# Reordering splits, exponentials and weight loads in a fused attention and two-mixture kernel

## The chip, the cores and the metric

The kernel runs on one core of a Trainium2 chip. The metric is the device time of one execution in microseconds; the time of a version is the median of its runs. The engines are named as in the profile: PE (TensorE, matrix products), PEld (its weight loads), DVE (VectorE), ACT (ScalarE), POOL (GpSimd), SP (SyncE, which issues most of the transfers). "SPq" and "ACTq" are transfers issued from the queues of SP and ACT.

## What is computed

Three stages follow each other, all in float32:

```python
# attention in chunks of 64, 8 batches x 8 heads x 576 positions x 64
scores = matmul(q_c, k_c^T) / 8
attn = exp(scores - max); attn /= sum(attn) + 1e-9
x = matmul(attn, v_c)                    # laid out as 4608 tokens x 512
# first mixture: 512 -> 2048 -> 512
h = x @ w_in
x = (h * clip(h + 3, 0, 6) / 6) @ w_out
# second mixture: 512 -> 1024 -> 512
h = x @ w_in2
s = h * softmax(h)
out = (layer_norm(s) * g_ln) @ w_out2
```

## The kernel before

**Precision.** Every float32 operand of a product is split into a rounded part `hi` (a ScalarE copy into a 1-pass type) and a remainder `lo` (a subtraction `lo = x - hi`, mostly on VectorE, here and there on GpSimd). A product is then three: hi*hi, lo*hi, hi*lo. So each product waits for one copy and one subtraction.

**The work in order.** The 4608 tokens are nine blocks of 512. Attention is done in 36 units of 128 tokens, spread between the products of the first mixture.

1. Blocks 0 to 2 run plainly. `moe_h` makes one 128-row piece of h (12 products), `moe_gate_there` applies the gate, `moe_split` makes `g_hi` and `g_lo`, and `o_next` (`moe_o`, 12 products) uses the piece made before. The loop `for F in range(2 * NF)` covers blocks 1 and 2, 32 steps. In odd F up to 25 an attention slot stands (`att_slot`: scores of the next unit into the one `att` bank, the values of the last one). A unit's eight exponentials (`attn_exp_act`, line 448, which read that bank) are done four in the odd F and four in the even F after it, from `STEPS`. Meanwhile `sums_of` (lines 1075 to 1083) and `split_sums` (lines 1089 and 1090) make sums of the weights for later and store them in DRAM (`sti`, `sto`); `UNITS` says in which F.
2. Blocks 3 to 8 are three pairs, with products in Strassen's form: seven products of half size instead of eight. `pair_7` does the first two pairs, `pair` the last.
   - The first half of `pair_7` has eight steps j. Each step multiplies in the order A11, S2, S1, S3, A12, then A22 and S4 of the step before (function `finish`), each of them six products in `mul7`, line 1164. VectorE adds s1, u2 (line 1373), u3 (line 1395) and c22 (line 1397); the gate and GpSimd follow and the results go into the groups B11, T1, B22, B21 of `wo` slots. Three further sums go to DRAM (`later_t`, line 1346).
   - The second half of `pair_7` makes seven outputs i with eight steps j each (`mul_o`, line 1301), d counts pairs of them. `prepare(d + 3)` splits operands (lines 1285 and 1286), `bring(d)` loads a sum back from `later_t` (line 1295). At j = 7 of the first two outputs stands an attention slot; its loads of values, queries and keys (lines 136, 129, 130) are issued one step later from SP's queue. The splits for the next pair come from the list `prep`, one at each of ten places; the eleventh (T4 in all but the first pair) is left over in `todo` and is done in the first step of the next pair.
   - `pair`, the last one, has the same seven products per step but runs output products plainly (`o_next`), stores halves of h in DRAM (`held`) and has the conversion of the second mixture's weights between: class `Second`, whose `window(words, small, hi)` scales a chunk on ScalarE (line 155), makes its words on VectorE (lines 258, 261, 267), starts the load of the chunk after next (line 145, two buffers `xr`), does small subtractions (lines 295, 302) and starts copies (line 319). `load_o` loads the second half of the block's weights from `sto` (line 1493).
3. The second mixture follows, with products by lines 751 and 949.

**What sets the order.** The kernel is written with a manual schedule: the order in the program is the order on each engine and on each DMA queue. An instruction that waits holds all that stand behind it on its engine. The weights of the pairs come through a ring of 16 pieces (`ring_fetch`, line 1151): each `mul7` and `mul_o` takes one and issues the next load into the freed place. The PSUM bank `b` of a step of `pair` is written by S2, added to by S3 and A22, and read by u2 (line 1522), u3 (line 1533) and c21 (line 1551) between these; the bank `a` is released by ramp and gate (lines 1230 and 550).

The order at the start of a step of `pair`, with what the change moves:

```python
mul7(b, j, "S2", "T2", True, False)
u2 = work_tile("s")
nc.vector.tensor_add(out=u2, in0=s1, in1=b)
if not j:
    fill.window(1, 0)
while todo:
    todo.pop(0)()
fill.window(1, 2)
c = h_psum()
mul7(c, j, "S1", "T1", True, False)
o_next()
mul7(b, j, "S3", "T3", False, False)
```

Of the kernel before, what the change touches and what calls it, by code (L numbers as in the profile page):

```python
# [21 lines left out]
def tile_kernel(  # L22
# [12 lines left out]
    nc = tc.nc  # L35
# [1224 lines left out]
    def home(name, m):  # L1260
        return wo_slot(GROUPS.index(name) * ND + m, F32)
# [26 lines left out]
        for k in range(2):  # L1288
            parts_o[i, 2 * m + k] = [t[k] for t in e]

    def bring(d):
        i, m = divmod(d, ND)
        if 0 <= i < 3:
            t = g_t[HOMES[i], m] = home(HOMES[i], m)
            nc.sync.dma_start(out=t, in_=later_t[i, m])

    def mul_o(ps, i, j, start, stop):
        w, x = ring_take("o", OUTS[i][0], j), parts_o.pop((i, j))
# [12 lines left out]
    def pair_7(p, todo):  # L1311
# [44 lines left out]
        for j in range(NJ):  # L1356
            u = base + event[j] if j in event else NU
            n = 2 * (j % 2)
            a = acc_bank(n) if j else att_psum()[:, 0]
            mul7(a, j, "A11", "B11", True, False)  # L1360
            s1 = work_tile("s")
            nc.scalar.copy(out=s1, in_=a)
            load_coming()
            while todo:
                todo.pop(0)()
            if late:
                gate_22(late[0])
            stage("turn", u)
            stage("exp", u + 1)
            b = acc_bank(n + 1) if j else h_psum()  # L1370
            mul7(b, j, "S2", "T2", True, False)
            u2 = work_tile("s")
            nc.vector.tensor_add(out=u2, in0=s1, in1=b)
            if j % 2 == 0:
                for g in GROUPS:
                    g_t[g, j // 2] = home(g, j // 2)
            m, k = j // 2, j % 2
            if j == 1:
                made = finish(*late, lambda: stage("norm", u + 1))
# [3 lines that stand above are left out]
            o_next()  # L1383
            if j > 1:
                made = finish(*late, lambda: stage("norm", u + 1))
            if j == NJ - 1:
                prepare(0)
            if made:
                i, t, ps = made
                gate(t, ps, t)  # L1390
                later_sums(i, t)
            if j != 1:
                mul7(b, j, "S3", "T3", False, False)
            u3 = ap1.tile([P, DM], F32, tag="tx2", name="tx2")
            nc.vector.tensor_add(out=u3, in0=s1, in1=b)  # L1395
            c22 = g_t["B22", m][:, k]
            nc.vector.tensor_add(out=c22, in0=u3, in1=c)
            mul7(a, j, "A12", "B21", False, True)
            t = gp_tile("t")
            ramp(a, t)  # L1400
            o_next()
            if u < NU:
                att_slot(u, u + 2, coming)
            if j == NJ - 1:
                prepare(1)
            gate(t, a, g_t["B11", m][:, k])
            late = j, b, c, s1, u2
# [15 lines left out]
        for i in range(len(OUTS)):  # L1423
# [7 lines left out]
            for j in range(NJ):  # L1431
                mul_o(ps, i, j, i in (0, 1, 3, 6), i in (2, 4, 5, 6))
                d = (i * NJ + j) // 2
                if (i, j) == (0, 5):
                    while waiting:
                        waiting.pop(0)()
                if j % 2:
                    bring(d)
                else:
                    prepare(d + 3)  # L1440
                if (i, j) in steps:
                    todo.pop(0)()
                u = base + 6 + i
# [9 lines left out]
                if final:  # L1453
                    if (i, j) == (5, 7):
                        second.append(Second())
                    elif (i, j) in ((6, 4), (6, 7)):
                        second[0].window(1, 0, False)
                    if j % 2 and d % 2 == 0 and d > 2 * ND:
                        load_o(d // 2 - ND - 1)
            for s in range(2):  # L1460
                if i == 0:
                    nc.scalar.copy(out=s1[s], in_=a[s])
# [34 lines left out]
    def pair(p, todo):  # L1497
        b1, b2 = FIRST + 2 * p, FIRST + 2 * p + 1
        hang, fill = None, second[0]
        for j in range(NJ):  # L1500
            lastj = j == NJ - 1
            if j == 1:
                width.update({"s": 3, "xo": 3})
                fill.places.append(3)
            if 2 * ND + 1 + j < NF:
                load_o(2 * ND + 1 + j)
            a = att_psum()[:, 0]
            mul7(a, j, "A11", "B11", True, False)
            s1 = work_tile("s")
# [1 line left out]
            if hang:  # L1511
                t, f = hang
                g = moe_split(t, nc.gpsimd)
                pend.append((b1, f, g))
            for _ in todo[:-1]:
                todo.pop(0)()
            if j:
                fill.window(1, 0)
            b = h_psum()
            mul7(b, j, "S2", "T2", True, False)  # L1520
            u2 = work_tile("s")
            nc.vector.tensor_add(out=u2, in0=s1, in1=b)
            if not j:
                fill.window(1, 0)
            while todo:
                todo.pop(0)()
            fill.window(1, 2)
            c = h_psum()
            mul7(c, j, "S1", "T1", True, False)
            o_next()  # L1530
# [4 lines left out]
            nc.vector.tensor_add(out=c22, in0=u3, in1=c)  # L1535
            if not lastj:
                nc.sync.dma_start(out=held[2 * j + 1], in_=c22)
            mul7(a, j, "A12", "B21", False, True)
            if lastj:
                for n in range(4):  # L1540
# [22 lines left out]
                nc.sync.dma_start(out=held[2 * j], in_=c12)  # L1563
            fill.store()
            hang = gated(c21), 2 * j + 1
        g = moe_split(hang[0], nc.vector)
        pend.append((b1, hang[1], g))

# [105 lines left out]
    for F in range(2 * NF):  # L1674
        b, f = 1 + F // NF, F % NF
        if F == 0:
            xn[2] = new_x()
        hp, t = moe_h(f, *xn[b])
        end = F == 2 * NF - 1
        (moe_gate if end else moe_gate_there)(hp, t)  # L1680
        if F - 2 in UNITS:
# [10 lines left out]
        if F < 2 * NF - 1:  # L1692
            o_next()
        for step, u, which in STEPS.get(F, []):
            if step == "exp":
                attn_exp_act(u, which)
            elif step in ("norm", "last"):
                if step == "norm":
                    attn_norm(u)
                attn_turn(u, which)  # L1700
# [145 lines left out]
```

## Time and profile before

| | |
|---|---|
| time, median of 3 runs | 1193.73 us (1192.16 to 1196.63) |
| the profiled execution's own time | 1193.68 us |
| its span, first to last instruction | 1192.0 us |
| PE busy | 1169.7 us, 98% |
| DVE, ACT, POOL busy | 75%, 61%, 41% |
| mean granted clock of PE | 0.996 |
| DRAM and SBUF transfers | 258.6 MB, 217 GB/s on the mean |

The profile is of one execution. The span leaves out what lies around the program, 1.7 us here. Busy PE is a modelled figure: products overlap, so a product of 392 ns takes its place in a row of products that is about 230 ns apart. The granted clock is 1.0 at 2.4 GHz and 0.5 at 1.2 GHz. Rows of a timeline give start and length in us, engine, line, operation, output and inputs, and in brackets the idle time of the engine before it and what ended that. What ended it is inferred; where several things were waited for, the last one by the profile is named.

### The profile page before, as it was taken

The numbers are of one execution on the slowest core, as the hardware profiler recorded it, in microseconds if no ns is written. First come the engines' busy times: TensorE is split into PE (matmuls) and PEld (weight loads), VectorE is DVE, ScalarE is ACT, GpSimd is POOL, SyncE is SP. The second block draws the span as 40 slices with busy tenths as digits, with TensorE's granted clock in tenths as the row PEclk, the third lists the DMA queues.
The fourth block names the chain that finished last, engine by engine and source line by source line (L and its number), as shares of the span: only waits on it lengthen the run. The fifth ranks groups of instructions, "written<-read, shape, count | busy, mean of one in ns | idle before, by whom it ended". The sixth has DMA issues, their size and how long they took to land.

```text
span 1192.0 us, 21417 instructions
## 1 busy us (share of the span) xinstructions
PE 1169.7 (98%) x7199; PEld 952.9 (80%) x7199; DVE 890.2 (75%) x1415; ACT 727.9 (61%) x1669; POOL 491.5 (41%) x565
## 2 busy tenths in 40 slices
PE   8999999999999999999999899999999999999998
PEld 6888778788888778787887788888888888888887
DVE  7987667677576987577866666678887878877874
ACT  7775545555465773366644333356886867777775
POOL 1000565443066610275500112101677676765764
PEclk9999999999999999999999899999999999999999
DMA  9901767777689997799999999862322222222311
GB/s 369 381 28 62 241 212 264 239 253 252 243 281 307 313 400 239 242 311 300 336 399 345 351 361 326 306 234 81 128 73 92 79 86 85 79 92 71 99 58 61
DMA packets 172253, 258.60 MB, mean 217 GB/s; under 512 B 19056, under 2 KB 86896, under 8 KB 172144
## 3 DMA queue, kind: packets, MB, share of 16 engines
q1 hardware_dynamic: 159760, 234.69, 57.2%
q10 hardware_dynamic: 12384, 22.55, 5.4%
q8 instruction: 57, 0.93, 0.3%
q14 instruction: 52, 0.43, 0.1%
HBM read 170.40 MB, written 76.02 MB: 207 GB/s over the span
## 4 chain that ended last, share of the span: by engine, by line
PE 91%; DVE 3%; DMA 2%; POOL 1%; ACT 1%; issue 1%; SPq 1%; ACTq 0%; POOLq 0%; DVEq 0%
PE acc L574 17%; PE po L949 16%; PE hp L535 9%; PE acc L1301 9%; PE hp L1164 9%; PE acc L1164 8%; PE b L751 6%; PE c L751 4%; PE a L751 4%; PE hp L1301 3%; PE att L398 3%; PE att L1164 2%; PE att L751 1%; POOL xo L1090 1%; DMA xr<-in_moe_w_in 1%
## 5 line engine op out<-in xcount | busy, mean ns | idle before, releaser
L574 PE MATMUL acc<-g_hi,wo 128*128 128x512 f32 x640 | 163.9, 395 | 0.0
L574 PEld LDWEIGHTS acc<-g_hi,wo 128*128 128x128 f32 x640 | 119.6, 189 | 26.6
L1164 PE MATMUL hp<-wi,w 128*128 128x512 f32 x468 | 119.1, 398 | 7.1 <-ACT wi L319 6.3
L1164 PEld LDWEIGHTS hp<-wi,w 128*128 128x128 f32 x468 | 89.2, 191 | 28.2 <-issue 6.7
L1164 PE MATMUL acc<-wi,w 128*128 128x512 f32 x420 | 104.4, 395 | 2.2 <-DVE tx L1395 2.2
L864 ACT COPY wo<-wo 32x256 f32<-32x256 f32 x228 | 92.1, 404 | 19.2 <-DVE wo L846 11.3
L535 PE MATMUL hp<-x_hi,wi 128*128 128x512 f32 x384 | 97.8, 396 | 0.1
L732 POOL TENSOR_TENSOR x_lo<-xr,x_hi 128x768 fp32r<-128x768 f32 (+1 forms) x30 | 64.1, 2157 | 76.4 <-ACT x_hi L725 76.4
L1301 PE MATMUL acc<-wi,w 128*128 128x512 f32 x408 | 95.3, 392 | 0.0
L1164 PEld LDWEIGHTS acc<-wi,w 128*128 128x128 f32 x420 | 77.9, 188 | 19.5 <-DVE tx L1395 2.5
L1301 PEld LDWEIGHTS acc<-wi,w 128*128 128x128 f32 x408 | 76.5, 188 | 16.8
L448 ACT ACTIVATE p<-att,mx 128x64 f32<-128x64 f32 x256 | 76.6, 320 | 18.8 <-DVE mx L431 16.0
L574 PE MATMUL acc<-g_lo,wo 128*128 128x512 f32 x320 | 87.7, 390 | 0.0
L535 PEld LDWEIGHTS hp<-x_hi,wi 128*128 128x128 f32 x384 | 71.5, 187 | 17.1 <-ACT x_hi L512 0.3
L1286 DVE TENSOR_TENSOR wi<-wo,wi 128x1024 fp32r<-128x1024 f32 x50 | 66.2, 1344 | 24.1 <-ACT wi L1285 23.6
L1285 ACT CAST wi<-wo 128x1024 fp32r<-128x1024 f32 x50 | 51.4, 1065 | 33.4 <-PE hp L1301 16.6
L836 DVE SCALAR_TENSOR_TENSOR wo<-wo,r,wo 128x1024 f32<-128x1024 f32 x36 | 70.3, 1952 | 1.3
L574 PEld LDWEIGHTS acc<-g_lo,wo 128*128 128x128 f32 x320 | 60.1, 188 | 12.8
L933 POOL TENSOR_TENSOR wo<-wo,wo 128x1024 fp32r<-128x1024 f32 x25 | 64.5, 2582 | 6.4 <-ACT wo L929 3.8
L560 POOL TENSOR_TENSOR g_lo<-t,g_hi 128x512 fp32r<-128x512 f32 x15 | 21.4, 1428 | 106.3 <-ACT g_hi L557 98.4
L828 ACT ACTIVATE wo<-wo,nmx 128x1024 f32<-128x1024 f32 x36 | 41.5, 1152 | 22.4 <-DVE nmx L825 22.3
L541 ACT ACTIVATE t<-hp,three 128x512 f32<-128x512 f32 x48 | 33.3, 694 | 35.0 <-PE hp L535 32.4
(319 smaller groups left out, 2848.5 us busy)
## 6 DMA issues: line engine op xcount, KB each, us to landing
w<-sti SPq DMA_DIRECT2D x168, 256.0 KB, 4.8
w<-sto SPq DMA_DIRECT2D x112, 256.0 KB, 5.2
later_t<-xo SPq DMA_DIRECT2D x48, 256.0 KB, 4.6
wo<-later_t SPq DMA_DIRECT2D x24, 512.0 KB, 6.9
wo<-wo SPq DMA_DIRECT2D x328, 32.0 KB, 1.8
x2d<-xo SPq DMA_DIRECT2D x36, 256.0 KB, 4.5
xr<-x2d SPq DMA_DIRECT2D x36, 256.0 KB, 3.3
out<-ob SPq DMA_DIRECT2D x36, 256.0 KB, 2.2
```

The source lines that it names most:

```text
L448: nc.scalar.activation(out=p_t[u][:, h], in_=sc[:, c, a], func=AF.Exp, scale=0.125, bias=mx[:, m : m + 1], accum_out=sums[u][:, h : h + 1],)
L535: nc.tensor.matmul(hp, wi[f][:, a, kk * P : (kk + 1) * P], b[:, kk], start=(n == 0), stop=(n == 3 * KD - 1),)
L574: nc.tensor.matmul(acc[dc], wo[f][:, w, dc * P : (dc + 1) * P], g[i], start=(at == 0 and n == 0), stop=(at == NF - 1 and n == 2),)
L732: eng.tensor_sub(out=lo[:, f], in0=r, in1=hi[:, f].bitcast(F32))
L751: nc.tensor.matmul(ps, x[:, AT[a], j], w2[w, j][i], start=(start and n == 0), stop=(stop and n == 5), skip_group_check=True,)
L836: nc.vector.scalar_tensor_tensor(out=h, in0=e, scalar=r, in1=h, op0=ALU.mult, op1=ALU.mult, accum_out=mu)
L864: move(out=m[b * 32 : b * 32 + 32, a], in_=tr[a * 32 : a * 32 + 32, b])
L933: eng.tensor_sub(out=lo, in0=m, in1=hi.bitcast(F32))
L949: nc.tensor.matmul(po, a[f], out_w[f][w], start=(n == 0), stop=(n == 3 * NF2 - 1),)
L1164: nc.tensor.matmul(ps, w[:, i, kk * P : (kk + 1) * P], x[:, kk], start=(start and n == 0), stop=(stop and n == 5), skip_group_check=True,)
L1286: nc.vector.tensor_sub(out=e[1], in0=src, in1=e[0].bitcast(F32))
L1301: nc.tensor.matmul(ps[s], w[:, k, s * P : (s + 1) * P], x[l], start=(start and j == 0 and n == 0), stop=(stop and j == NJ - 1 and n == 2), ...
```

## The change

- In `pair_7`, first half: what is left in `todo` is done behind u2, not ahead of the second product. At j = 7 `prepare(0)` stands behind c22, not ahead of the gate and u3.
- In `pair_7`, second half: the twelve loads from `later_t` were issued one per d in d = 0 to 11. Now they stand at d = 0, 2, 4, 6 (first sum), 8, 10, 12, 14 (second) and 16 to 19 (third), by the table `BRING_AT`.
- `load_o`: in the second pair nine were issued at even d from 10 to 26; now four at d = 21, 23, 25, 27. In `pair` one per step in seven steps became two per step in six.
- In `pair`, first step: what is left in `todo` follows u2 at once; the first window moves behind c22 and its store, the second to the end of the step. In later steps nothing moves. (The loop over `todo[:-1]` had nothing to do, since one entry is left.)
- In the loop over F: the second four exponentials of a unit, in even F, stand behind `moe_h` and ahead of the gate and of `moe_split`; they stood behind `o_next`. The first four, in odd F, stay.

```diff
--- before.py
+++ after.py
@@ -1288,11 +1288,12 @@
         for k in range(2):
             parts_o[i, 2 * m + k] = [t[k] for t in e]
 
-    def bring(d):
-        i, m = divmod(d, ND)
-        if 0 <= i < 3:
-            t = g_t[HOMES[i], m] = home(HOMES[i], m)
-            nc.sync.dma_start(out=t, in_=later_t[i, m])
+    def bring(i, m):
+        t = g_t[HOMES[i], m] = home(HOMES[i], m)
+        nc.sync.dma_start(out=t, in_=later_t[i, m])
+
+    BRING_AT = {2 * m: (0, m) for m in range(ND)} | {2 * (ND + m): (1, m) for m in range(ND)}
+    BRING_AT |= {4 * ND + m: (2, m) for m in range(ND)}
 
     def mul_o(ps, i, j, start, stop):
         w, x = ring_take("o", OUTS[i][0], j), parts_o.pop((i, j))
@@ -1361,8 +1362,6 @@
             s1 = work_tile("s")
             nc.scalar.copy(out=s1, in_=a)
             load_coming()
-            while todo:
-                todo.pop(0)()
             if late:
                 gate_22(late[0])
             stage("turn", u)
@@ -1371,6 +1370,8 @@
             mul7(b, j, "S2", "T2", True, False)
             u2 = work_tile("s")
             nc.vector.tensor_add(out=u2, in0=s1, in1=b)
+            while todo:
+                todo.pop(0)()
             if j % 2 == 0:
                 for g in GROUPS:
                     g_t[g, j // 2] = home(g, j // 2)
@@ -1383,8 +1384,6 @@
             o_next()
             if j > 1:
                 made = finish(*late, lambda: stage("norm", u + 1))
-            if j == NJ - 1:
-                prepare(0)
             if made:
                 i, t, ps = made
                 gate(t, ps, t)
@@ -1395,6 +1394,8 @@
             nc.vector.tensor_add(out=u3, in0=s1, in1=b)
             c22 = g_t["B22", m][:, k]
             nc.vector.tensor_add(out=c22, in0=u3, in1=c)
+            if j == NJ - 1:
+                prepare(0)
             mul7(a, j, "A12", "B21", False, True)
             t = gp_tile("t")
             ramp(a, t)
@@ -1434,10 +1435,10 @@
                 if (i, j) == (0, 5):
                     while waiting:
                         waiting.pop(0)()
-                if j % 2:
-                    bring(d)
-                else:
+                if j % 2 == 0:
                     prepare(d + 3)
+                elif d in BRING_AT:
+                    bring(*BRING_AT[d])
                 if (i, j) in steps:
                     todo.pop(0)()
                 u = base + 6 + i
@@ -1455,8 +1456,8 @@
                         second.append(Second())
                     elif (i, j) in ((6, 4), (6, 7)):
                         second[0].window(1, 0, False)
-                    if j % 2 and d % 2 == 0 and d > 2 * ND:
-                        load_o(d // 2 - ND - 1)
+                    if j % 2 and d >= 5 * ND and d % 2:
+                        load_o((d - 5 * ND) // 2)
             for s in range(2):
                 if i == 0:
                     nc.scalar.copy(out=s1[s], in_=a[s])
@@ -1502,8 +1503,9 @@
             if j == 1:
                 width.update({"s": 3, "xo": 3})
                 fill.places.append(3)
-            if 2 * ND + 1 + j < NF:
-                load_o(2 * ND + 1 + j)
+            for f in range(2 * j + ND, 2 * j + ND + 2):
+                if f < NF:
+                    load_o(f)
             a = att_psum()[:, 0]
             mul7(a, j, "A11", "B11", True, False)
             s1 = work_tile("s")
@@ -1512,19 +1514,16 @@
                 t, f = hang
                 g = moe_split(t, nc.gpsimd)
                 pend.append((b1, f, g))
-            for _ in todo[:-1]:
-                todo.pop(0)()
             if j:
                 fill.window(1, 0)
             b = h_psum()
             mul7(b, j, "S2", "T2", True, False)
             u2 = work_tile("s")
             nc.vector.tensor_add(out=u2, in0=s1, in1=b)
-            if not j:
-                fill.window(1, 0)
             while todo:
                 todo.pop(0)()
-            fill.window(1, 2)
+            if j:
+                fill.window(1, 2)
             c = h_psum()
             mul7(c, j, "S1", "T1", True, False)
             o_next()
@@ -1535,6 +1534,8 @@
             nc.vector.tensor_add(out=c22, in0=u3, in1=c)
             if not lastj:
                 nc.sync.dma_start(out=held[2 * j + 1], in_=c22)
+            if not j:
+                fill.window(1, 0)
             mul7(a, j, "A12", "B21", False, True)
             if lastj:
                 for n in range(4):
@@ -1563,6 +1564,8 @@
                 nc.sync.dma_start(out=held[2 * j], in_=c12)
             fill.store()
             hang = gated(c21), 2 * j + 1
+            if not j:
+                fill.window(1, 2)
         g = moe_split(hang[0], nc.vector)
         pend.append((b1, hang[1], g))
 
@@ -1676,6 +1679,9 @@
         if F == 0:
             xn[2] = new_x()
         hp, t = moe_h(f, *xn[b])
+        for step, u, which in STEPS.get(F, []):
+            if step == "exp" and F not in SLOT_AT:
+                attn_exp_act(u, which)
         end = F == 2 * NF - 1
         (moe_gate if end else moe_gate_there)(hp, t)
         if F - 2 in UNITS:
@@ -1692,7 +1698,7 @@
         if F < 2 * NF - 1:
             o_next()
         for step, u, which in STEPS.get(F, []):
-            if step == "exp":
+            if step == "exp" and F in SLOT_AT:
                 attn_exp_act(u, which)
             elif step in ("norm", "last"):
                 if step == "norm":
```

## Rows read from the trace of the kernel before

**Rows 1.** The page's first part, busy us, share and instructions of each engine.

```profile
PE 1169.7 (98%) x7199; PEld 952.9 (80%) x7199; DVE 890.2 (75%) x1415; ACT 727.9 (61%) x1669; POOL 491.5 (41%) x565
```

**Rows 2.** PE's waits: for whom, us in total, times, longest.

```profile
PE hp L1164 <- ACT wi L319: 6.3, 1, 6.3
PE att L398 <- ACT p L448: 2.7, 1, 2.7
PE acc L1164 <- DVE tx L1395: 2.2, 2, 1.1
...
PE att L398 <- DMA kbd<-in_k: 1.5, 1, 1.5
...
PE hp L1164 <- DVE s L1373: 0.8, 1, 0.8
```

**Rows 3.** Timelines of DVE, SP and PE, first step of the last pair.

```profile
652.52 0.69 DVE L261 SCALAR_TENSOR_TENSOR q<-xr,q 128x512 int32<-128x512 int32 x1 [0.34 <-ACT xr L155]
654.84 1.23 DVE L1182 TENSOR_TENSOR wi<-wi,wi 128x1024 fp32r<-128x1024 f32 x1 [1.63 <-ACT wi L1181]
656.30 0.43 DVE L258 TENSOR_SCALAR v<-xr 128x512 int32<-128x512 int32 x1 [0.23 <-DMA xr<-in_moe_w_in]
...
658.88 0.68 DVE L1533 TENSOR_TENSOR tx<-s,hp 128x512 f32<-128x512 f32 x1
...
656.34 1.95 SPq L145 DMA_DIRECT2D xr<-in_moe_w_out  x2
...
659.66 5.20 PE L1164 MATMUL hp<-wi,w 128*128 128x512 f32 x12 [6.27 <-ACT wi L319]
...
666.09 2.92 PE L1164 MATMUL hp<-wi,w 128*128 128x512 f32 x12
```

**Rows 4.** Stretches: busy us (instructions) of PE, PEld, DVE, ACT, POOL; clock, DMA share, GB/s.

```profile
646.35:664.70 18.35, 12.08 (x43) 9.44 (x42) 9.53 (x15) 6.65 (x10) 1.28 (x1) 0.81 1.04 393
646.35:770.30 123.95, 117.68 (x506) 96.38 (x505) 79.48 (x124) 45.74 (x76) 21.41 (x15) 0.97 0.95 343
424.00:438.00 14.00, 13.62 (x119) 11.35 (x120) 10.35 (x14) 11.69 (x30) 1.87 (x1) 1.00 1.04 409
```

**Rows 5.** DMA issues from 640 to 700 us: count, KB each, median us to landing.

```profile
xr<-in_moe_w_in SPq DMA_DIRECT2D x5, 512.0 KB, 5.7
```

**Rows 6.** Timeline, end of the first pair's first half.

```profile
394.09 1.22 DVE L1286 TENSOR_TENSOR wi<-wo,wi 128x1024 fp32r<-128x1024 f32 x1 [1.16 <-ACT wi L1285]
...
395.83 0.68 DVE L1395 TENSOR_TENSOR tx<-s,acc 128x512 f32<-128x512 f32 x1
...
396.56 1.66 PE L1164 MATMUL acc<-wi,w 128*128 128x512 f32 x6 [1.12 <-DVE tx L1395]
```

**Rows 7.** Timeline of DVE, first step of the second pair.

```profile
484.85 0.68 DVE L1373 TENSOR_TENSOR s<-s,hp 128x512 f32<-128x512 f32 x1
```

**Rows 8.** What SP's queue waited for: us in total, times, longest.

```profile
SPq L1295 <- DMA later_t<-xo: 4.8, 2, 2.5
```

**Rows 9.** Timeline of SP's queue, start of the first pair's second output.

```profile
417.01 0.32 SPq L1295 DMA_DIRECT2D wo<-later_t  x1
...
418.80 0.43 SPq L130 DMA_DIRECT2D kbd<-in_k  x1
```

**Rows 10.** The page's fifth part: busy us, mean ns of one, idle time before.

```profile
L448 ACT ACTIVATE p<-att,mx 128x64 f32<-128x64 f32 x256 | 76.6, 320 | 18.8 <-DVE mx L431 16.0
```

**Rows 11.** Timelines of ACT, DVE and PE in block 1, around its longest wait.

```profile
170.66 0.59 ACT L557 CAST g_hi<-hp 128x512 fp32r<-128x512 f32 x1 [2.45 <-DVE hp L545]
...
174.11 3.13 PE L574 MATMUL acc<-g_hi,wo 128*128 128x512 f32 x8
...
188.76 1.29 DVE L1075 TENSOR_TENSOR tx<-wi 128x512 f32<-128x512 f32 x2 [2.62 <-POOL xo L1090]
...
190.70 0.59 ACT L557 CAST g_hi<-hp 128x512 fp32r<-128x512 f32 x1 [2.85 <-DVE hp L545]
...
193.20 2.00 PE L574 MATMUL acc<-g_hi,wo 128*128 128x512 f32 x8
```

## The prediction

> **What bounds the kernel now.** I read the head of the page first: TensorE is busy for 98% of the span, the next engine for 75% [rows 1]. So a change can gain only where TensorE waits, or where it runs at the lower clock after a wait. The list of TensorE's waits is therefore the second view: behind the start-up there are five entries that matter, 6.3, 2.7, 2.2 (in two pieces), 1.5 and 0.8 us [rows 2], 13.5 us together. Each lies next to a place that the diff touches, and I take them one by one in the timeline. Durations come from the profiled execution: 1193.68 us, of which 1192.0 is the span. The median of the three runs is 1193.73 us, so a saving against the one is a saving against the other. About 0.5% (6.0 us) is what a measurement of this kernel can tell from no change.
>
> **1. The first step of the last pair.** TensorE resumes at 659.66 after 6.27 us [rows 3]. The wait is put down to a ScalarE copy, but the product A22 doesn't read what line 319 writes. It does overwrite the bank that the sum u3 (line 1533) reads, and this sum ran from 658.88 to 659.56 [rows 3], 0.1 us before the resumption. Why so late? VectorE works in order, and ahead of u3 stand the second mixture's words, whose operation at 656.30 waited for a transfer, and the T4 subtraction, at 654.84 [rows 3] because its ScalarE copy stood behind the same kind of work. The change puts T4 directly behind u2, one window behind c22 and the other at the end of the step. ScalarE's copy can then follow the copy of s1, the 1.23 us subtraction ends before S3 does, and u3 follows S3 at once. Saved: 6.27 us.
> The clock adds to this. Over that step the granted clock averages 0.81 [rows 4]; the 12 products behind the wait take 5.20 us, 12 such products later 2.92 [rows 3]: they ran at the lower of the two levels (1.2 instead of 2.4 GHz). Without the wait these 2.28 us go too. Sum 8.55 us.
> What is late next: the A bank, which the second step's first product overwrites. Its gate now stands behind u3, c22, two operations on words, a copy and the ramp: 0.68 + 0.68 + 0.43 + 0.69 by their like in [rows 3], and 0.69 each (an estimate, the size of those) for copy, ramp and gate, 4.55 us after S3. TensorE has A12, A22 and S4 meanwhile, 18 products: 4.4 us at 2.92 for 12, some 4.15 without the tail of the pipeline that each such group's time holds. I charge 0.4 us. **Part 1: 8.15 us**, bounds 4.2 (a new wait of middle size, below) and 8.55.
> The loads. Five of the nine 512 KB loads of later weights that stood in the second half move into the pair: two in each of six steps instead of one in each of seven, so one more load (two issues on SyncE's queue) stands ahead of the fill's load. At 393 GB/s [rows 4] that is 1.3 us per step. Before, the fill's load was issued at 656.34, 3.1 us after its buffer's words were read (652.52 + 0.69) [rows 3]; with 1.3 more it is 4.4, and it lands 5.7 us after issue [rows 5]: 10.1. In the second step I count 10.9 us from the buffer's reading to the point where it would delay u3: 72 products from S3 to A22 of the second step, 16.4 us without tails, less 2.5 before the reading and 3.0 for the fill's own operations (estimates from the same rows). Margin 0.8 us: thin, so I cost it at nothing but give it a rival. The ring of weights is fetched 16 pieces ahead and the moved weights are used three steps later; these have cover.
>
> **2. End of each pair's first half.** VectorE's 1.22 us subtraction of prepare(0) at 394.09, which waited for ScalarE, stood ahead of the gate and of u3 (395.83), and the late A22 began at 396.56, u3's end + 0.05 [rows 6]. Behind c22 the subtraction still ends near 396.4, and its first reader comes only after A22 and S4. Saved: both pieces, **2.2 us** [rows 2]; next is c22, early enough. Bounds 0 and 2.5.
>
> **3. The split at the start of a pair.** In the second pair u2 (484.85 [rows 7]) ran behind T4's subtraction, as long as the one in rows 3. In the new order u2 comes first, and S3 finds it done: **0.8 us** [rows 2]. The subtraction then fits before u3. In the first pair the same edit has no wait to remove. Bounds 0 and 0.9.
>
> **4. The sums' loads.** SyncE's queue waited for stores of later_t (4.8 us in two waits [rows 8]) and issued that load at 417.01, so the keys behind it went out at 418.80 [rows 9] and TensorE waited 1.5 us for them [rows 2]. In the new spread no such load stands in the last step of the first output, so the keys go out up to 2.5 us earlier (the longer wait of rows 8) and the 1.5 us are covered with 1.0 to spare. Saved: **1.5 us**, bounds 0 and 1.5. The twelve loads cost the same, each still at least five pairs of products ahead of its use.
>
> **5. The exponentials in the blocks.** The scores' wait of 2.73 us ended when the second four exponentials had read the bank. They ran behind the g_hi copy at 170.66, which had waited 2.45 us for VectorE's gate [rows 11]. Ahead of it they fill that idle time: four at 320 ns [rows 10] are 1.28 us, less than 2.45. So this wait goes, and the slow restart (8 products in 3.13 us at 174.11 against 2.00 at 193.20 [rows 11], 1.13 us) with it: 3.9 us at most. But the wait hides another one. GpSimd's subtraction releases VectorE's sums (188.76, after 2.62 us), the gate follows, and then the copy of g_hi at 190.70, which ends at 191.29 [rows 11]. Nothing of this chain starts from the moved exponentials: GpSimd's own row of sums and splits holds it, and TensorE's product at 193.20 needs that g_hi. It can come forward by 193.20 - 191.29 = **1.9 us**, no more; the rest turns into a few short waits for g_hi. Bounds 0 and 3.9.
>
> **Sum:** 8.15 + 2.2 + 0.8 + 1.5 + 1.9 = 14.55 us; 1193.7 - 14.6 = **1179.1 us**. All upper bounds: 17.35 us, 1176.3.
>
> **Would the transfers stand it?** The last pair moves 343 GB/s on average over 123.95 us [rows 4], 42.5 MB; with 2.6 MB more in 115.8 us it needs 390 GB/s. The rows show 393 in its first step and 409 GB/s over 14 us elsewhere [rows 4], so it just fits, and that is my sum.
> The Trainium skill ("DMA: Bandwidth & Descriptors", Where 436 GB/s comes from) speaks against it: for transfers between HBM and SBUF the HBM side binds at about 358 GB/s per core. The 409 GB/s above differ from that, and the measurement decides; by the page this stage would be bound by transfers, the third rival.
>
> **The rivals.**
> - **A late fill load** (0.25). The mechanism of part 1, one step on: the fill's load lands some us behind its place, ScalarE and VectorE stand, u3 is late. For it: the margin of 0.8 us, and a first step with 8.55 us less for its transfers. Against: two buffers, and a whole step between uses later on. Its price is that of the middle wait, 2.73 + 1.13 = 3.9 us, and some 0.5 more before other products: 1183.5 us.
> - **The exponentials are in the way** (0.07). Where the gate isn't late they delay g_hi, in 13 blocks by 1.28 us = 16.6 us: 1193.7 - 14.55 + 16.6 = 1195.7, no change. Against: ScalarE's idle time before that copy in rows 11, and TensorE has another block's products before it uses g_hi.
> - **The transfers bind the last pair** (0.05). If they went no faster than the pair's present average with 15 GB/s more, 358 GB/s, 45.1 MB would take 126.0 us, 2.0 more than now; with 6.4 saved elsewhere 1189.3.
> - **Slower** (0.05): the doubled loads make the fill late in several steps of the last pair, each a wait like the one removed, 8.55 us with its clock. From two on the gain of 14.55 is gone; three give 1193.7 - 14.55 + 25.65 = 1204.8. It decides where loads land over some 9 us behind their place (a step of 15 us less 5.7). Against: the 409 GB/s.
> - That an edit does nothing: each engine works in the program's order, so each edit does reorder; what may stay is the wait, and that is in the bounds.
>
> **How the numbers follow.** Forecast 0.58 (its own range 1176 to 1181.5), late fill 0.25; both are faster by over 0.5%: 0.83. Exponentials and bound transfers: 0.12 within. Slower 0.05. The range runs from all upper bounds, with 1 us more for restarts, to the late fill with parts 4 and 5 at their lower bounds: 1175 to 1187.
>
> **What the profile will show.** Right: no wait at the last pair's A22, granted clock 1.0 in its first step, T4's subtraction right behind u2; u3 ahead of prepare(0)'s subtraction; the keys' issue some 2.5 us earlier; exponentials ahead of the g_hi copy, and short waits for g_hi in the rounds of 178 and 191. Wrong: a wait at the second step's A22 with the fill's load as what released VectorE; transfers at a plateau below 390 GB/s through the pair; a block's wait of the old 2.7 us.

## The result, and the profile after

The changed kernel takes 1184.13 us (median of 4 runs, 1182.30 to 1184.61); the kernel before, on the same chip, 1193.80 us. The ratio is 0.9914, 95% interval 0.9892 to 0.9935: faster by 9.7 us, inside the range, but 5.0 us short of the forecast of 1179.1. The profiled execution took 1183.92 us with a span of 1181.8 us and a mean granted clock of 1.000. The first part of its page, against [rows 1]:

```profile
PE 1167.3 (99%) x7199; PEld 949.8 (80%) x7199; DVE 886.8 (75%) x1415; ACT 726.5 (61%) x1669; POOL 490.9 (42%) x565
```

TensorE's waits (for whom, us in total, times, longest), against [rows 2]:

```profile
PE hp L1164 <- DVE s L1522: 2.9, 3, 1.8
PE att L398 <- DVE pbd L494: 1.7, 2, 1.2
...
PE att L1164 <- DVE t L550: 0.5, 1, 0.5
PE acc L574 <- ACT g_hi L557: 0.4, 1, 0.4
PE hp L1164 <- DVE tx L1532: 0.3, 1, 0.3
```

All five entries of [rows 2] are gone. New ones took the place of two of them: VectorE's transposes (L494) in the block, and in the last pair u2 (now L1522), the A bank's gate (L550) and u3 (L1532).

Both kernels issue the same 7199 products in an order that can be matched, so the n-th product of one trace can be set against the n-th of the other. By how much a product starts earlier, and where that figure changes, gives the account:

| place (time before) | forecast, us | measured, us |
|---|---|---|
| start-up, not touched | 0 | 0.36 |
| block 1, 172 to 187 (part 5) | 1.9 | 1.32 |
| the late A22, 396.56 and 564.90 (part 2) | 2.2 | 1.19 + 1.27 |
| the keys, 424.38 (part 4) | 1.5 | 1.59 |
| second pair's u2, 485.58 (part 3) | 0.8 | 0.94 |
| last pair, first step, to 664.47 (part 1) | 8.55 | 8.73 |
| last pair, from 664.70 on (part 1) | -0.4 | -5.26 |
| sum | 14.55 | 10.14 |

The last row but one holds the error. The steps of part 1, in rows of the changed kernel; first the first step of the last pair, timelines of ACT, DVE and PE, against [rows 3]:

```profile
642.69 0.69 DVE L1522 TENSOR_TENSOR s<-s,hp 128x512 f32<-128x512 f32 x1 [2.12 <-PE hp L1164]
643.29 1.22 DVE L1182 TENSOR_TENSOR wi<-wi,wi 128x1024 fp32r<-128x1024 f32 x1
645.38 0.69 DVE L1532 TENSOR_TENSOR tx<-s,hp 128x512 f32<-128x512 f32 x1 [0.87 <-PE hp L1164]
646.55 2.92 PE L1164 MATMUL hp<-wi,w 128*128 128x512 f32 x12
649.94 1.66 PE L1164 MATMUL att<-wi,w 128*128 128x512 f32 x6 [0.47 <-DVE t L550]
```

u2, T4's subtraction and u3 follow each other as forecast; the twelve products behind A22 take 2.92 us, not 5.20, and TensorE then waits 0.47 us for the A bank's gate. What comes after that is the loss: products 0.64 us later at 649.94, 0.20 at 657.24, 0.52 at 663.00, 1.12 at 673.70, 2.23 at 690.98 and 0.49 at 736.64. The largest, in front of the fourth step's S3 (timelines of ACT, DVE and PE):

```profile
680.13 0.69 ACT L1230 ACTIVATE t<-att,three 128x512 f32<-128x512 f32 x1 [4.06 <-DMA st<-xo]
...
682.46 3.76 ACTq L326 DMA_DIRECT2D st<-wi  x4
...
682.66 0.68 DVE L1552 TENSOR_TENSOR tx<-s,hp 128x512 f32<-128x512 f32 x1
...
686.32 0.72 ACT L1230 ACTIVATE t<-tx,three 128x512 f32<-128x512 f32 x1 [4.12 <-issue]
...
687.08 0.69 DVE L550 SCALAR_TENSOR_TENSOR t<-t,tx 128x512 f32<-128x512 f32 x1 [3.14 <-ACT t L1230]
...
688.33 0.67 ACT L155 ACTIVATE xr<-xr 128x512 f32<-128x512 f32 x1
...
689.03 1.30 DVE L261 SCALAR_TENSOR_TENSOR v<-xr,v 128x512 int32<-128x512 int32 x1 [0.86 <-ACT xr L155]
...
690.25 0.68 DVE L1522 TENSOR_TENSOR s<-s,hp 128x512 f32<-128x512 f32 x1
...
690.98 1.65 PE L1164 MATMUL hp<-wi,w 128*128 128x512 f32 x6 [1.84 <-DVE s L1522]
```

Read it from the end: S3 waits for u2, which stands in VectorE's order behind the words of the second mixture and these behind the gate. The gate waits for the ramp on ScalarE, whose input (L1552) was there at 683.34 (682.66 + 0.68). From 682.46 to 686.22 four stores of second-mixture weights held ScalarE, which are no computation at all. The two smaller waits for u2 have the same chain: the ramps ahead of them, at 668.50 and 732.04, ran 2.4 and 3.1 us after their inputs (666.06 and 728.96), behind stores.

The row of four stores is not four long issues. Line 326's own records from 640 to 745 us (duration in ns: least, median, most), and below them what the issues of later weights waited for on SyncE's queue from 640 to 740 us:

```profile
L326 ACTq EVENT_SEMAPHORE  x29: 17/17/17, 659.3 to 742.2; - x29
L326 ACTq DMA_DIRECT2D st<-wi x16: 325/326/644, 660.2 to 742.4; - x16
...
SPq L1494 <- DMA w<-sti: 9.4, 12, 2.1
```

An issue takes 0.33 to 0.64 us; the rest is waiting for a semaphore (a counter by which a transfer tells that it has landed). The operands in the trace say which: all transfers from the queues of SyncE and ScalarE share eight semaphores in turn, and each of the 1175 that follow another on theirs was issued after that one had landed. So at most eight are under way; from 680 to 695 us it was 7.9 on the mean. Three of the four stores went out within 0.08 us of the landing of a load of later weights that SyncE had issued 6.1 to 6.6 us before. A store on ScalarE thus waits for loads that it has nothing to do with. It is so in every run here; GpSimd's transfers, where there are any, use eight semaphores of their own.

The wait at 663.00 has another cause, the fill's load (timelines of DVE, SP and PE):

```profile
647.23 0.69 DVE L261 SCALAR_TENSOR_TENSOR q<-xr,q 128x512 int32<-128x512 int32 x1
...
653.41 0.38 SPq L145 DMA_DIRECT2D xr<-in_moe_w_out  x1
...
659.15 0.43 DVE L258 TENSOR_SCALAR p<-xr 128x512 int32<-128x512 int32 x1 [2.31 <-DMA xr<-in_moe_w_out]
...
663.00 3.03 PE L1164 MATMUL hp<-wi,w 128*128 128x512 f32 x12 [0.35 <-DVE tx L1532]
```

The load went out 5.5 us after its buffer had been read (647.92) and landed 11.2 us after; VectorE's words waited for it and u3 stood behind them.

The transfers in the four steps after the first (busy us and instructions of PE, PEld, DVE, ACT, POOL; clock, DMA share, GB/s), against [rows 4]:

```profile
649.94:665.00 15.06, 14.71 (x63) 11.65 (x64) 11.97 (x20) 5.98 (x10) 2.60 (x3) 1.00 1.06 392
665.00:680.10 15.10, 14.28 (x63) 11.41 (x62) 8.78 (x14) 5.22 (x9) 2.92 (x2) 1.00 1.02 372
680.10:697.00 16.90, 15.06 (x66) 11.95 (x65) 9.68 (x15) 6.28 (x11) 2.90 (x2) 1.00 1.05 384
697.00:712.10 15.10, 15.10 (x67) 12.40 (x67) 9.51 (x16) 6.06 (x10) 2.59 (x2) 1.00 1.06 397
```

The other parts, in timelines of ACT, DVE, PE and SP: the block, the end of the first pair's first half, and the keys, against [rows 11, 6, 9]:

```profile
170.48 0.89 DVE L494 STREAM_TRANSPOSE pbd<-p 32x256 f32<-32x256 f32 x2
170.49 0.58 ACT L557 CAST g_hi<-hp 128x512 fp32r<-128x512 f32 x1 [1.29 <-DVE hp L545]
...
171.43 0.68 PE L398 MATMUL att<-pbd,v 64*64 64x64 f32 x28 [1.20 <-DVE pbd L494]
...
178.25 2.12 PE L574 MATMUL acc<-g_hi,wo 128*128 128x512 f32 x8 [0.39 <-ACT g_hi L557]
...
392.08 0.68 DVE L1394 TENSOR_TENSOR tx<-s,acc 128x512 f32<-128x512 f32 x1
...
393.40 1.22 DVE L1286 TENSOR_TENSOR wi<-wo,wi 128x1024 fp32r<-128x1024 f32 x1
...
393.69 1.65 PE L1164 MATMUL acc<-wi,w 128*128 128x512 f32 x6
...
413.31 0.33 SPq L130 DMA_DIRECT2D kbd<-in_k  x1
```

### The profile page after: what moved, and what is told of

It is laid out like the page before. It is cut to its first block, busy times and chain, and to the rows that moved or that the text cites. A ratio compares the mean times of both kernels' runs of the same rounds, so it can differ in the third digit from the quotient of the medians.

```text
span 1181.8 us, 21412 instructions
## 1 busy us (share of the span) xinstructions
PE 1167.3 (99%) x7199; PEld 949.8 (80%) x7199; DVE 886.8 (75%) x1415; ACT 726.5 (61%) x1669; POOL 490.9 (42%) x565
## 4 chain that ended last, share of the span: by engine, by line
PE 86%; DMA 5%; DVE 4%; POOL 1%; ACT 1%; issue 1%; SPq 0%; ACTq 0%; POOLq 0%; DVEq 0%
PE po L949 17%; PE acc L574 14%; PE acc L1302 9%; PE hp L535 9%; PE acc L1164 8%; PE hp L1164 6%; PE b L751 6%; PE hp L1302 4%; PE c L751 4%; PE a L751 4%; PE att L398 3%; DMA xr<-in_moe_w_out 2%; PE att L751 1%; PE att L1164 1%; DMA wo<-sto 1%
```

## The experiments

All ran against the kernel before on the same chip (medians of before 1193.8 us for e1 to e4, 1194.6 for e5 to e8, 1194.8 for e9 and e10). "Nets" is what the last pair gains by matched products, first step and loss together; each is from one profile. How far such a figure carries, e4 and e8 show: they leave the last pair as in the changed kernel, and it nets 3.71 and 4.14 us there, against 3.47.

**e1: the weight loads as before.** The forecast had costed one more load per step at nothing; was that the loss?

```diff
-            for f in range(2 * j + ND, 2 * j + ND + 2):
-                if f < NF:
-                    load_o(f)
+            if 2 * ND + 1 + j < NF:
+                load_o(2 * ND + 1 + j)
...
-                    if j % 2 and d >= 5 * ND and d % 2:
-                        load_o((d - 5 * ND) // 2)
+                    if j % 2 and d % 2 == 0 and d > 2 * ND:
+                        load_o(d // 2 - ND - 1)
```

> The changed kernel with the weight loads for the last pair (line 1494) put back to where they stood: nine in the second pair's second half, one in each of seven steps of the last pair. All else as changed. In the changed kernel the last pair's steps lost about 5.2 us to waits (0.47, 0.35, 0.82 and 1.84 us of idle time and the restarts behind them). Theory 1, the doubled loads keep the transfers at their ceiling (392 to 397 GB/s in five steps) and so hold up ScalarE's own stores and the fill's loads: the pair loses at most 1.5 us, time 1180 to 1181. Theory 2, the first step is 8.7 us shorter and the transfers lag for that reason alone, with either schedule: the same waits stay, 1183 to 1185. Theory 3, no waits from transfers at all, the order on VectorE is what holds u2: unchanged, 1184.

Measured 1183.02 us (1181.48 to 1184.32), ratio 0.991 (0.9895 to 0.9925). The pair nets 3.85 us against 3.47. Of the 0.4 us more nothing can be said. The long wait for u2 is still there, 2.83 us at 690.61, by the same chain (timelines of ACT and DVE):

```profile
679.81 6.04 ACTq L326 DMA_DIRECT2D st<-wi  x4
...
685.96 0.73 ACT L1230 ACTIVATE t<-tx,three 128x512 f32<-128x512 f32 x1 [6.00 <-DMA st<-wi]
686.72 0.69 DVE L550 SCALAR_TENSOR_TENSOR t<-t,tx 128x512 f32<-128x512 f32 x1 [5.01 <-ACT t L1230]
```

So the moved loads alone were not the cause: without them the four stores hold ScalarE for 6.04 us instead of 3.76. The time fits theory 2.

**e2: the second mixture's stores from SyncE's queue.**

```diff
-                    nc.scalar.dma_start(out=st2[OPERANDS.index(name)][:, i], ...)
+                    nc.sync.dma_start(out=st2[OPERANDS.index(name)][:, i], ...)
```

> The changed kernel with the second mixture's weight stores (line 326) issued from SyncE's queue instead of ScalarE's. If the path of the loss is ScalarE standing at the issue of its stores while the transfers are full (four stores took 3.76 us at 682.46 and the ramp behind them ran at 686.32, 3 us after its input was there), the wait of 1.84 us at u2 of the fourth step goes and that of the third step (0.82) too: time 1181 to 1182.5. If the path is the late load of the fill alone, the waits stay or grow, since SyncE's queue gets 6 more issues in a step: 1184 to 1187.

Measured 1183.16 us (1182.40 to 1185.05), ratio 0.9917 (0.99 to 0.9933), between the two ranges. The waits for u2 go, and one of 2.85 us at u3 of the third step comes: a ScalarE copy into a place whose store had not finished waited 7.82 us (the store now stood in SyncE's queue behind a `held` store), and VectorE's words and u3 waited behind it. The pair nets 4.2 us. One wait was traded for another.

**e3: the order of `pair` alone**, all else as before (part 1 without its loads).

> The kernel before with one part of the change alone: the new order in the steps of the last pair (the left-over split behind u2, the two windows of the first step later); loads as before, exponentials, prepare(0) and the sums' loads as before. Theory 1 (the doubled loads cost the rest): gains 7.5 to 8.5 us, 1185.3 to 1186.3. Theory 2 (less transfer time in the first step): gains 3.5 to 5 us, 1189 to 1190.3. The forecast's own term for this part was 8.15.

Measured 1188.63 us (1187.00 to 1191.65, 5 runs), ratio 0.996 (0.9945 to 0.9974). The profiled execution was the slowest of the five, 1191.65 us. In it the first step gains 8.74 us and 5.30 of them are lost again, 4.9 by the end of the pair; the median gains 5.2 in all. No other part of the change is in this kernel, so most of the loss belongs to the reorder itself. What a first step that is 8.7 us shorter does to the transfers can be read in the 15 us behind it: in the kernel before, 5.4 of the eight possible transfers were under way there on the mean, in e3 7.3. That this missing time to catch up makes the loss is argued from it; no run gave the time back.

**e4: the exponentials back** behind `o_next`.

> The changed kernel with the exponentials of the even steps put back behind the output products. The forecast's term for this part was 1.9 us; the two traces show 1.35. If the exponentials in front of the split cost nothing elsewhere, the scores' wait of 2.7 us with its slow restart comes back and the time is 1.0 to 1.9 us more: 1185.1 to 1186.0. If they hold up g_hi somewhere in the other twelve blocks, the time is the same or less: 1183 to 1184.1.

Measured 1185.43 us (1184.72 to 1188.82), ratio 0.9936 (0.9919 to 0.9953), 1.3 us above the changed kernel, as the first theory said. The old wait is back, 2.74 us at 172.20, and the slow products behind it.

**e5: the stores of h to `held` left out.** This kernel leaves out fourteen stores of 256 KB and reads other data in their place, so its output is not the reference's; it has less to transfer.

```diff
-            if not lastj:
-                nc.sync.dma_start(out=held[2 * j + 1], in_=c22)
...
-            else:
-                nc.sync.dma_start(out=held[2 * j], in_=c12)
```

> The changed kernel without the 14 stores of h halves in the last pair (lines 1536 and 1564, 256 KB each, two per step, 0.5 of about 5.8 MB of a step); the loads that read them take finished rows of another buffer instead, so the last block's output is left out. Theory A, after the first look: through the first five steps of the last pair the transfers run at their ceiling (372 to 397 GB/s), ScalarE stands at the issue of the second mixture's stores and holds the sums of h behind it; with a tenth less to move the waits of 5.2 us in the pair fall below 2 us, time 1179.5 to 1181.5, and the stretch 712 to 727 drops well below 390 GB/s. Theory B, the new order on ScalarE and VectorE makes those waits by itself: they stay, 1183.5 to 1184.5.

Measured 1185.83 us (1182.78 to 1186.24), ratio 0.9922 (0.9904 to 0.9941), above both ranges. The waits stay: 0.48, 0.86 and 2.25 us at the same three places, the last followed by a stretch at a granted clock of 0.94, which neither theory had priced. Four stores still hold ScalarE for 5.58 us. A tenth less to transfer does not help.

**e6: the same stores from GpSimd's queue**, an engine that is busy for 2.9 of the 16.9 us from 680.10 (windows above).

```diff
-                    nc.scalar.dma_start(out=st2[OPERANDS.index(name)][:, i], ...)
+                    nc.gpsimd.dma_start(out=st2[OPERANDS.index(name)][:, i], ...)
```

> The changed kernel with the second mixture's stores (line 326) issued from GpSimd's queue. GpSimd is busy for 2.9 of a step's 15 us and what it makes (g_lo) is needed a third of a step later, so a stand at the issue costs less there, and the stores don't stand behind SyncE's queue as in the run with stores on SyncE, where one landed 7.8 us late for the copy that reuses its place. Theory A: the wait at u2 of the fourth step (1.84 us) goes and no other takes its place, time 1180.5 to 1182. If the late landing of the stores counts and not where they are issued, a wait of 2 to 3 us stands elsewhere, as on SyncE: 1183 to 1184.

Measured 1182.74 us (1181.34 to 1183.14), ratio 0.99 (0.9885 to 0.9914), between the two ranges. ScalarE is free, yet one long wait of 2.79 us stays, at u2 in front of the fourth step's S3. Its cause is another (timelines of SP, POOL and DVE):

```profile
661.38 0.39 SPq L145 DMA_DIRECT2D xr<-in_moe_w_in  x1
...
673.87 0.43 DVE L258 TENSOR_SCALAR p<-xr 128x512 int32<-128x512 int32 x1 [2.64 <-DMA xr<-in_moe_w_in]
673.87 3.44 SPq L1494 DMA_DIRECT2D wo<-sto  x4
...
678.91 0.35 SPq L145 DMA_DIRECT2D xr<-in_moe_w_in  x1
...
680.71 2.16 POOL L326 DMA_DIRECT2D st<-wi  x4
...
688.13 0.43 DVE L258 TENSOR_SCALAR v<-xr 128x512 int32<-128x512 int32 x1 [6.20 <-DMA xr<-in_moe_w_in]
```

The four issues take 2.16 us on GpSimd, 0.54 each and none held. Now the fill's load (L145) is late. Its buffer had been read at 670.11, but it goes out at 678.91, behind four issues of later weights. These could begin only when the fill's load before it, issued at 661.38, had landed at 673.85, and took 3.44 us with the waits between them (0.36 to 0.37 each by itself). It lands at 688.11, and VectorE's words wait 6.20 us for it. That is the mechanism of the late-fill rival. In the changed kernel the same load landed at 687.72, when the words came only at 687.74 because of the held ScalarE: there the one hid the other.

**e7: both**, the stores on GpSimd (e6) and the loads as before (e1).

> Both: stores from GpSimd's queue and the weight loads as they stood before the change (nine early, one per step). The one left waits at the first product of the second step and u2 of the fourth, the other at several; with both the fewest bytes lie in the pair and ScalarE is free. Theory A: 1179.5 to 1181, the pair's waits below 1.5 us in sum. If early loads only move the same backlog ahead of the pair: 1182 to 1183.

Measured 1181.69 us (1180.84 to 1183.10), ratio 0.9894 (0.9875 to 0.9912). The time lies between the two ranges. The pair nets 7.05 us; two waits are left in it, 0.54 us at u2 of the first step and 0.47 at the A bank.

**e8: the sums' loads as before**, one per d from 0 to 11, the rest as changed.

> The changed kernel with the loads of the sums back at d = 0 to 11. The forecast's term for this part was 1.5 us and the traces show 1.6: the wait for the keys comes back, 1.5 to 1.8 us, and with a slow restart up to 3.2 us. The last pair begins with the same or a smaller backlog, since nothing stands at d = 16 to 19, so up to 1 us may come back there: time 1184.7 to 1186.5. If the spread had no part in the gain, 1184.

Measured 1186.76 us (1184.07 to 1187.99), ratio 0.9932 (0.9912 to 0.9952), a little more than I allowed for; its profile is of its fastest execution, 1184.07. The wait for the keys is back, 1.48 us at 421.00. From 612 to 623 us only 166 GB/s are moved, 356 in the changed kernel, and the last pair still waits 0.47, 0.36, 1.55 and 0.47 us: fewer transfers ahead of the pair don't help it either.

**e9 and e10: the two loads per step in the middle of the step**, behind the store of c22, no longer at its start. In e9 the stores are on GpSimd, in e10 on ScalarE. The transfers are those of the changed kernel; only their place in the queues differs.

```diff
-            for f in range(2 * j + ND, 2 * j + ND + 2):
-                if f < NF:
-                    load_o(f)
             a = att_psum()[:, 0]
...
             if not lastj:
                 nc.sync.dma_start(out=held[2 * j + 1], in_=c22)
+            for f in range(2 * j + ND, 2 * j + ND + 2):
+                if f < NF:
+                    load_o(f)
```

> The version with the stores of the second mixture on GpSimd's queue, with the two loads of later weights per step of the last pair moved from the step's start to behind the store of c22. Theory (the fill's load came late because it stood behind four issues of these loads in SyncE's queue): the wait of 2.8 us at u2 of the third step goes, the fill's loads go out within 1 us of their words being read, and the time is 1180 to 1182 us. Rival (the transfers are at their ceiling, so it does not matter in which order they are asked for): the fill's load still takes over 6 us to land, a wait of 1.5 to 3 us stays in the second or third step, and the time is 1182 to 1184.

> The changed kernel with the two loads of later weights per step of the last pair moved from the step's start to behind the store of c22, the second mixture's stores left on ScalarE. Theory (ScalarE stands at the issue of its stores while the transfers are at their ceiling, and that alone is enough for a late u2): four issues on ScalarE still take 3 us or more in the third step, u2 there waits 1.5 us or more, and the time is 1183 to 1185 us. Rival (the queue of loads alone was the cause): the waits of the last pair go but for two of 0.5 us, and the time is 1180 to 1182.

e9: 1181.02 us (1180.37 to 1181.77), ratio 0.9889 (0.9872 to 0.9905). One wait of the last pair is left, and the pair nets 7.47 us: 8.65 in the first step, 1.18 lost. The theory's other sign failed: of the fourteen fill's loads only four went out within 1 us of their buffer being read, the others 1.1 to 5.6 us after it. But none came too late for u2 or u3. Its timelines of POOL, ACT and DVE around the start of the fourth step, and its transfers:

```profile
680.65 2.16 POOL L326 DMA_DIRECT2D st<-wi  x4
681.27 0.72 ACT L1230 ACTIVATE t<-tx,three 128x512 f32<-128x512 f32 x1 [2.28 <-DVE tx L1552]
...
686.20 0.67 DVE L1519 TENSOR_TENSOR s<-s,hp 128x512 f32<-128x512 f32 x1
```

```profile
650.00:665.00 15.00, 14.40 (x61) 11.03 (x61) 11.97 (x20) 5.41 (x10) 4.87 (x6) 1.00 1.06 404
665.00:680.00 15.00, 15.00 (x67) 12.37 (x66) 11.41 (x19) 7.16 (x12) 8.12 (x11) 1.00 1.05 404
680.00:695.00 15.00, 15.00 (x67) 12.34 (x67) 9.14 (x14) 5.96 (x10) 7.60 (x12) 1.00 1.05 408
```

The ramp now runs at 681.27, while the stores are being issued elsewhere, and u2 ends at 686.87, 1.6 us ahead of S3 (688.50). TensorE is busy throughout the two later stretches.

e10: 1185.72 us (1184.63 to 1185.99), ratio 0.9926 (0.9911 to 0.9941), 0.7 us above what the theory allowed. The four stores on ScalarE (timeline of ACT) are back in the way, and u2's wait of 3.09 us was followed by a granted clock of 0.84 from 680 to 695 us and 0.93 from 695 to 710, which cost 2.7 us more:

```profile
681.28 5.26 ACTq L326 DMA_DIRECT2D st<-wi  x4
686.65 0.72 ACT L1230 ACTIVATE t<-tx,three 128x512 f32<-128x512 f32 x1 [5.69 <-DMA st<-wi]
```

**Together.** What the last pair nets, by the place of stores and loads, with the ratio:

| | loads at the step's start | loads as before | loads in the middle |
|---|---|---|---|
| stores on ScalarE | 3.47 (0.9914) | 3.85 (0.991) | 1.23 (0.9926) |
| stores on GpSimd | 3.89 (0.99) | 7.05 (0.9894) | 7.47 (0.9889) |

Neither row nor column does it alone. The last two cells of the lower row, and only these, hold nearly the whole forecast of 8.15. 3.47, 3.85 and 3.89 can't be told apart, nor can 7.05 and 7.47. e9 is the fastest of all the versions; against the changed kernel its median is 3.1 us lower, while the two intervals overlap (0.9872 to 0.9905, 0.9892 to 0.9935). By the times alone only e9 against e10 is clear of noise (0.9905 and 0.9911): the place of the stores. That the place of the loads counts too rests on the profiles: e6's wait of 2.79 us is gone in e7 and e9.

## Why the prediction was right in direction and 5 us too low

**Parts 2, 3 and 4 were right**, steps and sizes: 2.46, 0.94 and 1.59 us measured for 2.2, 0.8 and 1.5. u3 runs ahead of prepare(0)'s subtraction (392.08 and 393.40). The keys go out at 413.31 instead of 418.80, 5.5 us earlier, of which 2.9 are the shift of everything there, so 2.6 by the change itself: the 2.5 of [rows 8].

**Part 5** had the right step and too large a size: 1.32 us by matched products, 1.3 by e4, not 1.9. The wait for the exponentials went, and g_hi was not what alone came next. I had looked only at ScalarE's and GpSimd's chain; VectorE's transposes of the weights p (L494) took 1.20 and 0.52 us of it, g_hi 0.39.

**Part 1's first step was right**: 8.73 us measured for 8.55, clock included, and the A bank's gate 0.64 for 0.4.

**What failed is the term for the loads in part 1, "so I cost it at nothing"**, and with it the sentence that the transfers "just fit". In its place stand 5.26 - 0.64 = 4.6 us. It was not the one load more per step: e1 and e3 lose about as much without it. The volume did fit: e9 moves the same bytes at 404 to 408 GB/s and waits only for the A bank's gate. What did not fit was where engines stand while eight transfers are under way, and I had looked at one such place where there are two:

- ScalarE issues the stores of the second mixture and waits before an issue until an earlier transfer has landed: 3.76 us with the four at 682.46 of the changed kernel, 6.04 in e1. Ramp, gate, words and u2 stand behind it. In the changed kernel it is what the three waits for u2 show, 1.12 + 2.23 + 0.49 = 3.8 us; at the 2.23 the fill's load came as late, as e6 shows. I had counted issues on SyncE's queue only.
- SyncE's queue waits in the same way ahead of the fill's load. I had it go out 4.4 us after its buffer's reading and land after 10.1, with a margin of 0.8 us. It went out after 5.5 and landed after 11.2, and the second step's A22 waited 0.35 us for u3: the sign that I had named as wrong. The next three landed 13.0, 15.2 and 15.8 us after the reading.

e6 and e10 remove one each and the other shows; e9 removes both. Since e9 has the new order and nets 7.47 us, the order by itself is not the cause. Why the loss came only now, e3 suggests: the old 6.27 us wait had also been time in which transfers caught up. Whether more than eight under way would do as well as moving the stores was not tried.

**The rivals.** The late fill load gave 1183.5 us, and 1184.1 came. That it came so near is in good part luck: its mechanism is there, at 663.00 and in e6, but in the changed kernel it cost 0.5 us by itself, and 3.8 stand behind ScalarE's stores, which no rival had. The exponentials were not in the way. Transfers did not bind the pair by their rate: the Trainium skill ("DMA: Bandwidth & Descriptors", Where 436 GB/s comes from) puts the HBM side at about 358 GB/s per core, and the runs here show 404 to 408 GB/s for 45 us on end in e9, so the measurement decides. The slower rival's several waits did come, three at u2 with 2.9 us in all and one each at u3 and the A bank, though only the one at u3 by a late fill; it had priced each at 8.55 us and was wrong in that: without a fall of the clock they cost 0.5 to 2.2 us each.

## What to carry to other kernels

A wait that is taken away may also have been time for transfers. Where transfers are always under way, look at what each engine that issues them has queued behind the issue, since it may stand there for microseconds until some other queue's transfer has landed; a row of several issues hides that, so look at the single records. Stores belong on the queue of an engine with nothing urgent behind them, and loads with slack behind the load that has none. And a change that nets half of its forecast may have two causes, each hiding the other: remove both before ruling one out.

## What the runs showed of the hardware that I had not expected

- **An issue is short; the wait before it is not.** Four stores of 256 KB on ScalarE's queue held it for 3.76, 6.04, 5.58 and 5.26 us (changed kernel, e1, e5, e10) at 369 to 393 GB/s, with 0.33 to 0.64 us for an issue itself and the rest for the landing of earlier transfers. The same four on GpSimd's took 2.16, 2.39 and 2.16 us (e6, e7, e9) at 401 to 410 GB/s without a wait between them.
- **With more under way, each takes longer to land.** From 680 to 695 us 7.9 transfers were under way on the mean in the changed kernel, 11.7 in e9, where the stores are outside the eight. The fill's loads for the words of the fourth step landed 6.5 and 7.3 us after their issue in the one, 9.0 and 9.7 in the other.
- **The rate held.** Transfers ran at 400 to 410 GB/s over 15 us stretches in e7 and e9.
- **The clock's fall after a wait was not regular.** After waits of 2.74 (e4), 2.25 (e5), 2.15 (e3) and 3.09 us (e10) the granted clock fell to its lower level for some us: on the mean 0.57 over the 4 us behind the wait in e4, 0.94 and 0.84 over the 15 us from 680 in e5 and e10. After 2.85 (e2), 2.83 (e1) and 2.79 us (e6) it stayed at 1.00. What decides was not tried.
